# A two-product feed-forward kernel: both products read their moving tile in turns from its two halves, and part of the activation moves from VectorE to ScalarE

## The chip, the cores and the metric

The kernel runs on one core of one Trainium2 chip. A core has a matrix engine (TensorE, in the profile PE, its weight loads PEld), VectorE (DVE), ScalarE (ACT), GpSimd (POOL) and SyncE (SP, which issues transfers here). The engines run their own queues in order and wait for each other by semaphores. SBUF is the working memory, PSUM the memory that TensorE writes and from which VectorE and ScalarE read. The metric is device time in microseconds for one launch.

## The reference

`x` has 8 sequences of 4096 tokens with 192 channels, 32768 tokens in all. A causal convolution of 7 taps (softmax weights, one set for each of 8 groups of channels) is followed by a feed-forward layer with 2048 hidden values:

```python
x = lightconv(x, weight)            # (32768, 192), 7 taps per channel group
h = x @ w_in                        # 192 -> 2048
g = np.where(h >= 1, h, np.where(h <= -1, 0, (h + 1) ** 2 / 4))
out = g @ w_out                     # 2048 -> 192
```

With c = min(max(h, -1), 1), g is max(h, ((c + 1) / 2)^2). The same g comes out of min(relu((h + 1) / 2)^2, 1), and then the larger of that and h.

## The kernel before

The tokens are cut into 64 tiles of 512 (`TB`), and the hidden values into 8 groups of 256 (`NPAIR`). A step `q` is one tile `s` and one group `j` (q = 8 s + j), 512 steps in all. In step q TensorE gets the first product of q (`mm1`, into a PSUM tile `h` of 2 x 512 columns) and then the second product of q - 2 (`mm2`, into four PSUM accumulators `accm0`, `accm1`, `accr0`, `accr1`, which collect over the eight groups of a tile). Hidden values lie on the partitions, tokens are the columns, and the weights are the stationary operand.

From tile 2 on, every operand is split into a rounded part and a remainder, both fp32r (`hi`, `lo` of x; `gh`, `gl` of g; two parts of each weight). The products of the parts are summed in PSUM. The 192 channels are 128 and 64: the tiles with `r` in their names hold the last 64. Each matmul uses 64 of the 128 rows, and matmuls for the upper and the lower 64 rows stand alternately. A step has 18 matmuls of `mm1` and 20 of `mm2`, each with 512 moving columns. Tiles 0 and 1 differ: tile 0 uses plain f32 for the first product while the weights are still being split, tile 1 fp32r; the second product of both runs as `mm2_first` in f32 with 192 moving columns.

Between the products stand, for a step q:

- `act_clip` (VectorE, PSUM to SBUF): the clip to -1 and 1, into a tile `g`,
- `act_square` (ScalarE): ((c + 1) / 2)^2 in place,
- `act_max` (VectorE): the maximum with h, after which h's buffer (there are two) is free,
- `act_hi` (ScalarE) and `act_lo` (VectorE), issued in step q + 1: the rounded part `gh` and the remainder `gl`.

`both_square` and `most` form g in another way, and tile 0 uses them (part of its first step aside): a relu and a square on ScalarE, and one VectorE instruction for the minimum with 1 and the maximum with h.

After the eighth group of a tile, `evac` copies the four accumulators to SBUF on ScalarE (tiles `t`), GpSimd adds them in pairs into `sum`, `evac_rest` folds the upper and lower half of the 64 last channels, and `store` transposes blocks of 32 on VectorE and sends them out. `evac_last` does the last tile with transposes on TensorE. The accumulators have one buffer each. Beside all this the convolution of coming tiles is spread over the steps (`conv_slot`, by hand-written plans): products with the taps on ScalarE (L219), sums on GpSimd (L230), transposes on VectorE (L147).

The order on every engine is the order of the code: the schedule is manual, and the main loop writes it out.

Of the kernel before, what the change touches and what calls it, by code (L numbers as in the profile page):

```python
# [13 lines left out]
AF = mybir.ActivationFunctionType  # L14
# [4 lines left out]
P = 128  # L19
TB = 512  # L20
# [10 lines left out]
def lightconv_then_ffn(ctx: ExitStack, tc: tile.TileContext, x, weight, w_in, w_out, out):  # L31
# [24 lines left out]
    nc = tc.nc  # L56
    B, S, D = x.shape
# [7 lines left out]
    NPAIR = NF // 2  # L65
    DR = D - P
    NG = TB // SQ + 1
    TOP, BOT = slice(0, DR), slice(DR, P)
    HALVES = (TOP, BOT)
# [62 lines left out]
    NF32 = 2 * NPAIR  # L132
# [169 lines left out]
    ident = const.tile([P, P], F32, name="ident")  # L302
# [87 lines left out]
    NQ = NSB * NPAIR  # L390
    hs, g32, gs, ghs, gls, accs = {}, {}, {}, {}, {}, {}

    def mm1(q):

        s, j = divmod(q, NPAIR)

        if q == 0:
            h = hs[q] = [ps_o.tile([P, TB], F32, name=n) for n in ("accr1", "accm0")]
        else:
            h = hs[q] = ps_h.tile([P, 2, TB], F32, name="h")  # L400
            h = [h[:, e, :] for e in range(2)]

        if s == 0:
            mms = [(WI[j], us, [xop[s][u] for u in us]) for us in ("ns", "sn", "rr")]
        else:
            mms = [(W[j][:, part], u + u, [xop[s][u, x]] * 2) for u in "nsr"
                   for part, x in ((0, "hi"), (1, "hi"), (0, "lo"))]
        for n, (w, us, x) in enumerate(mms):
            for e in range(2):
                c0 = COL[us[e]][e]  # L410
                nc.tensor.matmul(h[e], w[HALVES[e], c0:c0 + P], x[e][e],  # L411
                                 start=(n == 0), stop=(n == len(mms) - 1))

    def new_accs(s):
        accs[s] = {(a, i): ps_o.tile([P, TB], F32, name=f"acc{a}{i}")
                   for a in "mr" for i in range(2)}
# [16 lines left out]
    def mm2(q):  # L433

        s, j = divmod(q, NPAIR)
        gh, gl = ghs.pop(q), gls.pop(q)
        w, wr, k = W[j + LAG], WR[j + LAG], n_in[j + LAG]
        if j == 0:
            new_accs(s)
        m0, m1, r0, r1, r = ("m", 0, gh), ("m", 1, gh), ("m", 0, gl), ("r", 0, gh), ("r", 0, gl)  # L440
        mms = [(e, m) for ms in ((m0, m1), (r0,), (r1,), (r,)) for e in range(2) for m in ms]
        if q == NQ - 1:
            mms = [(0, m) for m in (r1, m0, m1, r, r0)] + [(1, m) for m in (r1, r, m0, m1, r0)]
        first = {a: min(n for n, (e, m) in enumerate(mms) if m[0] == a) for a in "mr"}
        last = {a: max(n for n, (e, m) in enumerate(mms) if m[0] == a) for a in "mr"}
        for n, (e, (a, part, g)) in enumerate(mms):
            c0 = k + e * P
            for i in range(2):
                st = (w[HALVES[i], part, c0:c0 + P] if a == "m"
                      else wr[HALVES[i], e].rearrange("p a d -> p (a d)"))  # L450
                nc.tensor.matmul(accs[s][a, i], st, g[HALVES[i], e, :],  # L451
                                 start=(j == 0 and n == first[a]),
                                 stop=(j == NPAIR - 1 and n == last[a]))


    def tiles(q):
        return [slice(0, 1), slice(1, 2)] if q == NQ - 1 else [slice(0, 2)]

    def act_clip(q):
        g = gs[q] = act.tile([P, 2, TB], F32, name="g", bufs=3)  # L460
        for e in tiles(q):
            nc.vector.tensor_scalar(out=g[:, e, :], in0=hs[q][:, e, :], scalar1=-1.0, scalar2=1.0,  # L462
                                    op0=ALU.max, op1=ALU.min)

    def act_square(q):
        g = gs[q]
        for e in tiles(q):
            nc.scalar.activation(g[:, e, :], g[:, e, :], AF.Square, bias=0.5, scale=0.5)  # L468

    def act_max(q):  # L470
        h, g = hs.pop(q), gs[q]
        for e in tiles(q):
            nc.vector.tensor_tensor(out=g[:, e, :], in0=h[:, e, :], in1=g[:, e, :], op=ALU.max)  # L473
        if q < NF32:
            g32[q] = gs.pop(q)
# [14 lines left out]
    def evac(s):  # L490

        acc = accs.pop(s)
        n = slice(0, 2 * D if s * NPAIR < NF32 else TB)
        for a in "mr":
            t = [ob.tile([P, TB], F32, name="t", bufs=4) for _ in range(2)]
            y = ob.tile([P, TB], F32, name="sum")
            nc.scalar.copy(t[0][:, n], acc[a, 0][:, n])
            nc.scalar.copy(t[1][:, n], acc[a, 1][:, n])  # L498
            if s > 0:
                nc.gpsimd.tensor_add(y[:, n], t[0][:, n], t[1][:, n])  # L500
            else:
                late.append((y[:, n], t[0][:, n], t[1][:, n]))
            sums[s, a] = y
# [32 lines left out]
    def evac_last(s):  # L536


        acc = accs.pop(s)
        half, rest = slice(0, TB // 2), slice(TB // 2, TB)  # L540
        part = {}
        for a in "rm":
            u, v = [ob.tile([P, TB], F32, name="t", bufs=4) for _ in range(2)]
            for n in (half, rest):
                nc.scalar.copy(u[:, n], acc[a, 0][:, n])
                nc.vector.tensor_tensor(out=v[:, n], in0=acc[a, 1][:, n], in1=u[:, n], op=ALU.add)
            part[a] = v
        ps = [ps_h.tile([P, 2, TB], F32, name="h")[:, 0] for _ in range(2)]
        ps += [ps_o.tile([P, TB], F32, name=f"accr{i}") for i in range(2)]
        y = [ob.tile([P, TB], F32, name="sum") for _ in range(2)]  # L550
        for b in range(TB // P):
            nc.tensor.matmul(ps[b][:, P:D], part["r"][:, b * P:(b + 1) * P], ident[:, 0:DR],  # L552
                             start=True, stop=True)
        for i in range(2):
            for b in (2 * i, 2 * i + 1):
                nc.tensor.transpose(ps[b][:, 0:P], part["m"][:, b * P:(b + 1) * P], plain)
            for b, copy in ((2 * i, nc.scalar.copy), (2 * i + 1, nc.vector.tensor_copy)):
                copy(y[i][:, b % 2 * D:(b % 2 + 1) * D], ps[b][:, 0:D])
                if i == 1:
                    (nc.sync if b % 2 else nc.scalar).dma_start(  # L560
                        out=out[s * TB + b * P:s * TB + (b + 1) * P],
                        in_=y[i][:, b % 2 * D:(b % 2 + 1) * D])
            if i == 0:
                nc.sync.dma_start(
                    out=out[s * TB:s * TB + 2 * P].rearrange("(b p) d -> p b d", p=P),
                    in_=y[i][:, 0:2 * D].rearrange("p (b d) -> p b d", b=2))
# [180 lines left out]
    def most(h, g):  # L747

        nc.vector.scalar_tensor_tensor(out=g, in0=g, scalar=1.0, in1=h, op0=ALU.min, op1=ALU.max)
# [75 lines left out]
    for q in range(NQ + DELAY):  # L825
        s, j = divmod(q, NPAIR)
        c, i = divmod(q, 2 * NPAIR)
# [11 lines left out]
        if q < NQ:  # L839
            mm1(q)  # L840
# [7 lines left out]
        else:  # L848
            if q - 1 in gs:
                act_hi(q - 1)  # L850
            if q == NPAIR + 1:
                evac(0)
            if q == 2 * NPAIR - 2:
                pending.extend(late)
            if q < NQ:
                let_go()
                act_clip(q)
                act_square(q)
            if done % NPAIR == NPAIR - 1 and done >= NPAIR:
                (evac if done < NQ - 1 else evac_last)(done // NPAIR)  # L860
# [4 lines left out]
            if q < NQ:  # L865
                let_go()
                act_max(q)
                parts_lo(q, (False,))
                conv_slot(i, conv_b, conv_n.get("a"), conv_n.get("r"))

            m, r = (DELAY, DELAY + 1) if s > 1 else (NPAIR - 2, NPAIR - 1)
# [7 lines left out]
        if q == NQ - 4:  # L879
            plain = ob.tile([P, TB // SQ, SQ], F32, name="osb").rearrange("p j b -> p (j b)")[:, 0:P]  # L880
# [27 lines left out]
```

## Time and profile before

| | |
|---|---|
| runs | 2235.05 us median of 3 (2235.0 to 2235.06) |
| profiled execution | span 2233.2 us from first to last instruction; the page gives no other time of its own, and the median of the runs is 1.85 us above it |
| TensorE busy | 2227.3 us (100%), 19646 matmuls |
| VectorE busy | 2093.3 us (94%) |
| ScalarE busy | 1693.7 us (76%) |
| GpSimd busy | 1173.8 us (53%) |
| DMA | 110.84 MB, mean 50 GB/s |

Busy time is the union of an engine's instructions. Since matmuls overlap and their ends are modelled, the length of a matmul is better read from the starts of two groups than from a row's mean. The page's part on the chain follows, from the last instruction back, what each step waited for.

### The profile page before, as it was taken

To read this page: it belongs to the slowest core of one execution; us is meant where nothing else is said; L and a number is where in the kernel's file an instruction comes from. 1 tells how busy PE (TensorE), PEld (TensorE's weight loads), DVE (VectorE), ACT (ScalarE), POOL (GpSimd) and SP (SyncE) were. 2 spreads that over 40 slices of the span, in tenths; PEclk is the share of its full clock that TensorE was granted. 3 is DMA by queue.
4 is the path that set the end of the run, shared out by engine and by line. 5 is a ranking of instruction groups with operands and counts; after the bars stand their busy time and mean duration, and the time that the engine had idled before them with its cause. 6 is when DMAs were issued, how large, how long until landed. Compare 5 with 4: busy or idle time off the path is not lost.

```text
span 2233.2 us, 48204 instructions
## 1 busy us (share of the span) xinstructions
PE 2227.3 (100%) x19646; PEld 1850.7 (83%) x19646; DVE 2093.3 (94%) x1883; ACT 1693.7 (76%) x2153; POOL 1173.8 (53%) x868
## 2 busy tenths in 40 slices
PE   9999999999999999999999999999999999999999
PEld 6988888888888888888888888888888888888887
DVE  8899999999999999999999999999999999999998
ACT  7677877778777787777877777877778777787775
POOL 1456644556545565455664456644556545565451
PEclk9999999999999999999999999999999999999999
DMA  6222222221222212222122222222221222212211
GB/s 160 49 52 48 42 47 47 52 53 39 52 49 46 54 34 52 49 49 51 40 47 48 49 51 50 41 49 46 50 54 39 52 49 46 54 34 52 49 34 25
DMA packets 442125, 110.84 MB, mean 50 GB/s; under 512 B 410288, under 2 KB 417840, under 8 KB 441904
## 3 DMA queue, kind: packets, MB, share of 16 engines
q1 hardware_dynamic: 441744, 107.66, 24.5%
q8 instruction: 155, 2.54, 0.5%
q14 instruction: 66, 0.54, 0.1%
q10 hardware_dynamic: 160, 0.10, 0.0%
HBM read 32.84 MB, written 25.17 MB: 26 GB/s over the span
## 4 chain that ended last, share of the span: by engine, by line
PE 99%; ACT 0%; DMA 0%; DVE 0%; issue 0%; DVEq 0%; ACTq 0%
PE h L411 47%; PE accm L451 30%; PE accr L451 20%; PE accr L429 1%; PE accm L429 1%; PE accr L190 0%; PE accr L411 0%; DMA osb<-in_weight_dram 0%; PE accm L181 0%; PE h L552 0%; ACT xT L168 0%; ACT xT L165 0%; ACT xT L167 0%; PE accm L411 0%; PE h L155 0%
## 5 line engine op out<-in xcount | busy, mean ns | idle before, releaser
L230 POOL TENSOR_TENSOR y<-y,p 128x512 f32<-128x512 f32 x546 | 798.2, 1462 | 733.3 <-DVE g L473 560.7
L411 PE MATMUL h<-hi,w 64*128 64x512 f32 x4032 | 764.7, 387 | 0.0
L486 DVE TENSOR_TENSOR gl<-g,gh 128x1024 fp32r<-128x1024 f32 (+1 forms) x497 | 730.4, 1470 | 29.3 <-ACT gh L480 24.2
L468 ACT ACTIVATE g<-g 128x1024 f32<-128x1024 f32 (+1 forms) x505 | 535.5, 1061 | 234.8 <-DVE g L462 228.5
L480 ACT CAST gh<-g 128x1024 fp32r<-128x1024 f32 (+1 forms) x497 | 522.8, 1052 | 226.8 <-DVE g L473 185.2
L462 DVE TENSOR_SCALAR g<-h 128x1024 f32<-128x1024 f32 (+1 forms) x505 | 609.1, 1206 | 85.5 <-PE h L411 84.4
L451 PE MATMUL accm<-gh,w 64*128 64x512 f32 x3968 | 639.6, 387 | 0.0
L473 DVE TENSOR_TENSOR g<-h,g 128x1024 f32<-128x1024 f32 (+1 forms) x505 | 613.3, 1215 | 11.8 <-ACT g L468 4.5
L411 PEld LDWEIGHTS h<-hi,w 64*128 64x128 f32 x4032 | 561.3, 185 | 75.4
L411 PE MATMUL h<-lo,w 64*128 64x512 f32 x2016 | 613.0, 387 | 0.0
L451 PEld LDWEIGHTS accm<-gh,w 64*128 64x128 f32 x3968 | 463.6, 184 | 75.6
L451 PE MATMUL accr<-gh,wr 64*128 64x512 f32 x1984 | 414.8, 387 | 0.0
L451 PE MATMUL accr<-gl,wr 64*128 64x512 f32 x1984 | 414.8, 386 | 0.0
L451 PE MATMUL accm<-gl,w 64*128 64x512 f32 x1984 | 414.7, 387 | 0.0
L411 PEld LDWEIGHTS h<-lo,w 64*128 64x128 f32 x2016 | 371.3, 184 | 38.1 <-DMA lo<-lo 0.2
L219 ACT ACTIVATE p<-xT,wk 128x512 f32<-128x512 f32 x562 | 374.9, 709 | 0.0
L451 PEld LDWEIGHTS accm<-gl,w 64*128 64x128 f32 x1984 | 276.4, 184 | 37.9
L451 PEld LDWEIGHTS accr<-gh,wr 64*128 64x128 f32 x1984 | 276.3, 184 | 37.8
L451 PEld LDWEIGHTS accr<-gl,wr 64*128 64x128 f32 x1984 | 276.2, 184 | 37.9
L411 PE MATMUL h<-rhi,w 64*128 64x512 f32 x992 | 304.1, 386 | 0.0
L411 PE MATMUL h<-rh,w 64*128 64x512 f32 x992 | 304.1, 386 | 0.0
L500 POOL TENSOR_TENSOR sum<-t 128x512 f32<-128x512 f32 (+1 forms) x124 | 157.4, 1291 | 101.8 <-ACT t L498 101.8
(143 smaller groups left out, 1945.4 us busy)
## 6 DMA issues: line engine op xcount, KB each, us to landing
out_dram<-osb SPq DMA_DIRECT2D x366, 64.0 KB, 1.9
raw<-in_x_dram SPq DMA_DIRECT2D x334, 68.0 KB, 2.4
hi<-hi SPq DMA_DIRECT2D x126, 128.0 KB, 2.3
lo<-lo SPq DMA_DIRECT2D x126, 128.0 KB, 2.3
rhi<-rh SPq DMA_DIRECT2D x62, 128.0 KB, 2.2
rlo<-rl SPq DMA_DIRECT2D x62, 128.0 KB, 2.3
words<-in_moe_w_in_dram SPq DMA_DIRECT2D x16, 192.0 KB, 3.6
words<-in_moe_w_out_dram SPq DMA_DIRECT2D x8, 384.0 KB, 4.8
```

The source lines that it names most:

```text
L219: nc.scalar.mul(p, self.xT[:, SH + k:SH + k + TB], wk[:, self.wsel, k:k + 1])
L230: nc.gpsimd.tensor_add(y, y, self.product(k))
L411: nc.tensor.matmul(h[e], w[HALVES[e], c0:c0 + P], x[e][e], start=(n == 0), stop=(n == len(mms) - 1))
L429: nc.tensor.matmul(accs[s][a, i][:, c0:c0 + D], g[half, e, b * P:(b + 1) * P], w[half, e, :], start=(j == 0 and e == 0 and b % 2 == 0), st ...
L451: nc.tensor.matmul(accs[s][a, i], st, g[HALVES[i], e, :], start=(j == 0 and n == first[a]), stop=(j == NPAIR - 1 and n == last[a]))
L462: nc.vector.tensor_scalar(out=g[:, e, :], in0=hs[q][:, e, :], scalar1=-1.0, scalar2=1.0, op0=ALU.max, op1=ALU.min)
L468: nc.scalar.activation(g[:, e, :], g[:, e, :], AF.Square, bias=0.5, scale=0.5)
L473: nc.vector.tensor_tensor(out=g[:, e, :], in0=h[:, e, :], in1=g[:, e, :], op=ALU.max)
L480: nc.scalar.copy(gh[:, e, :], gs[q][:, e, :])
L486: eng.tensor_sub(gl[:, e, :], g[:, e, :], gh[:, e, :])
L500: nc.gpsimd.tensor_add(y[:, n], t[0][:, n], t[1][:, n])
```

## The change

Two things are done together.

First, the moving operand. `turns` views the 512 columns of a tile as two halves of 256 and takes column 0 of the first, column 0 of the second, column 1 of the first, and so on. The output is still written in order, so its columns stand in that mixed order. `mm1` does this from tile 2 on, `mm2` for every tile from 2 on. After both products a column n = 4 a + 2 b + o of an accumulator is token 256 b + 128 o + a, and `evac` writes it back to its place: it reads the PSUM columns in order and writes each to its token's column in `t`, 128 columns apart from one to the next. For the last tile, the transposes in `evac_last` take every fourth column instead.

Second, the activation. In steps 3, 4 and 11 to 15 of every sixteen (from tile 2 on, without the last two steps) ScalarE forms relu((h + 1) / 2) and its square, and VectorE one `most`, in place of clip, square and maximum.

```diff
+    def turns(t):
+        return t.rearrange("p (o c) -> p c o", o=2)
+    def both(t):
+        return t.rearrange("p (c o) -> p c o", o=2)
+    def in_turns(s):
+        return s * NPAIR >= NF32
...
     def mm1(q):
-                nc.tensor.matmul(h[e], w[HALVES[e], c0:c0 + P], x[e][e],
+                to, of = (both(h[e]), turns(x[e][e])) if in_turns(s) else (h[e], x[e][e])
+                nc.tensor.matmul(to, w[HALVES[e], c0:c0 + P], of,
...
     def mm2(q):
-                nc.tensor.matmul(accs[s][a, i], st, g[HALVES[i], e, :],
+                nc.tensor.matmul(both(accs[s][a, i]), st, turns(g[HALVES[i], e, :]),
...
+    BY_ACT = (3, 4, 11, 12, 13, 14, 15)
+    def by_act(q):
+        return q % (2 * NPAIR) in BY_ACT and NF32 <= q < NQ - 2
     def act_clip(q):
         g = gs[q] = act.tile([P, 2, TB], F32, name="g", bufs=3)
+        if by_act(q):
+            nc.scalar.activation(g, hs[q], AF.Relu, bias=0.5, scale=0.5)
+            return
...
     def act_square(q):
+        if by_act(q):
+            nc.scalar.activation(g, g, AF.Square)
+            return
...
     def act_max(q):
-        for e in tiles(q):
+        if by_act(q):
+            most(h, g)
+        for e in () if by_act(q) else tiles(q):
...
     def evac(s):
-            nc.scalar.copy(t[0][:, n], acc[a, 0][:, n])
-            nc.scalar.copy(t[1][:, n], acc[a, 1][:, n])
+            for i in range(2):
+                to, of = t[i][:, n], acc[a, i][:, n]
+                if in_turns(s):
+                    to = to.rearrange("p (b o a) -> p a b o", b=2, o=2)
+                    of = of.rearrange("p (a b o) -> p a b o", b=2, o=2)
+                nc.scalar.copy(to, of)
...
     def evac_last(s):
-            nc.tensor.matmul(ps[b][:, P:D], part["r"][:, b * P:(b + 1) * P], ident[:, 0:DR],
+            nc.tensor.matmul(ps[b][:, P:D], part["r"][:, b::TB // P], ident[:, 0:DR],
...
-                nc.tensor.transpose(ps[b][:, 0:P], part["m"][:, b * P:(b + 1) * P], plain)
+                nc.tensor.transpose(ps[b][:, 0:P], part["m"][:, b::TB // P], plain)
```

TensorE, GpSimd and SyncE keep their instructions in the same order. On ScalarE, around an evacuation in the middle of the kernel, stood before (the four copies of the accumulators in step 9 of sixteen, then the rounding to `gh`, the square, two conv products and the fold of the `r` sum in step 10, then step 11):

```order
L497 COPY t<-accm_14124 128x512
L498 COPY t<-accm_14125 128x512
L497 COPY t<-accr_14126 128x512
L498 COPY t<-accr_14127 128x512
L480 CAST gh<-g 128x1024
L468 ACTIVATE g<-g 128x1024
L219 ACTIVATE p<-xT,wk 128x512 x2
L510 COPY t<-sum 64x512
L480 CAST gh<-g 128x1024
L468 ACTIVATE g<-g 128x1024
L219 ACTIVATE p<-xT,wk 128x512 x2
```

And now, at the same place (line numbers are those of the changed kernel; L479 is the relu, L488 its square):

```order
L527 COPY t<-accm_14124 128x128x4
L527 COPY t<-accm_14125 128x128x4
L527 COPY t<-accr_14126 128x128x4
L527 COPY t<-accr_14127 128x128x4
L505 CAST gh<-g 128x1024
L491 ACTIVATE g<-g 128x1024
L219 ACTIVATE p<-xT,wk 128x512 x2
L539 COPY t<-sum 64x512
L505 CAST gh<-g 128x1024
L479 ACTIVATE g<-h 128x1024
L488 ACTIVATE g<-g 128x1024
L219 ACTIVATE p<-xT,wk 128x512 x2
```

The copies write four interleaved pieces of 128 columns, and in step 11 the relu stands between the rounding and the square; it reads `h`, and so waits for the first product itself.

On VectorE, from the end of step 10 (the transpose of the `m` sum that `store` issues) to step 12, stood before the clip (L462), the remainder (L486) and the maximum (L473) of each step:

```order
L523 STREAM_TRANSPOSE osb<-sum 128x512
L462 TENSOR_SCALAR g<-h 128x1024
L486 TENSOR_TENSOR gl<-g,gh 128x1024
L473 TENSOR_TENSOR g<-h,g 128x1024
L523 STREAM_TRANSPOSE osb<-sum 64x512
L462 TENSOR_SCALAR g<-h 128x1024
L486 TENSOR_TENSOR gl<-g,gh 128x1024
L473 TENSOR_TENSOR g<-h,g 128x1024
```

And now:

```order
L552 STREAM_TRANSPOSE osb<-sum 128x512
L511 TENSOR_TENSOR gl<-g,gh 128x1024
L778 SCALAR_TENSOR_TENSOR g<-g,h 128x1024
L552 STREAM_TRANSPOSE osb<-sum 64x512
L511 TENSOR_TENSOR gl<-g,gh 128x1024
L778 SCALAR_TENSOR_TENSOR g<-g,h 128x1024
```

The clip is gone from these steps, and one instruction of the form of `most` stands where the maximum stood. There are 215 such steps.

## The prediction

> **What bounds the kernel now.** I read the page first, then the granted clock, then the chain in order of time, then the matmuls' starts, and last the engines that might come to wait. From the page:
>
> ```profile
> span 2233.2 us, 48204 instructions
> PE 2227.3 (100%) x19646; PEld 1850.7 (83%) x19646; DVE 2093.3 (94%) x1883; ACT 1693.7 (76%) x2153; POOL 1173.8 (53%) x868
> PE 99%; ACT 0%; DMA 0%; DVE 0%; issue 0%; DVEq 0%; ACTq 0%
> ```
>
> TensorE carries 99% of the chain that ended last. VectorE is 94% busy, though, so a faster TensorE could soon wait for it. The view of cores gives the clock, the chain in order of time gives the length of a step (one step is 18 matmuls of the first product, L411, then 12 and 8 of the second, L451):
>
> ```profile
> core 0: 2233.2 us, clock 1.000
> 268.10 2.04 PE h L411 x18
> 270.14 1.36 PE accm L451 x12
> 271.50 0.91 PE accr L451 x8
> ...
> 281.02 2.04 PE h L411 x18
> ```
>
> The clock is never throttled, so nothing is to be won there. Three steps take 281.02 - 268.10 = 12.92 us, one 4.307 us. A step has 38 matmuls of 64 rows, which run as 19 pairs side by side (upper and lower half of the array): 4307 / 19 = 226.7 ns for a pair. TensorE's instructions follow each other without a gap; only the length of a pair is left to shorten.
>
> How long would a pair have to be? The first tile's steps use plain f32 operands in place of the rounded ones (fp32r), and the timeline of TensorE there shows:
>
> ```profile
> 33.08 1.91 PE L411 MATMUL h<-hi,gl 64*128 64x512 f32 x8
> 34.79 1.05 PE L411 MATMUL h<-rh,gl 64*128 64x512 f32 x4
> 35.65 0.85 PE L429 MATMUL accm<-wf,g 64*128 64x192 f32 x8
> ...
> 38.25 1.91 PE L411 MATMUL h<-hi,gl 64*128 64x512 f32 x8
> 39.97 1.05 PE L411 MATMUL h<-rh,gl 64*128 64x512 f32 x4
> 40.83 0.85 PE L429 MATMUL accm<-wf,g 64*128 64x192 f32 x8
> ```
>
> Twelve matmuls of 512 columns (six pairs) take 35.65 - 33.08 = 2.57 and 40.83 - 38.25 = 2.58 us: 429.2 ns a pair. Thirty-two of 192 columns (four rows of eight, 16 pairs) take 38.25 - 35.65 = 2.60 us: 162.5 ns a pair. The difference of 266.7 ns over 320 columns is 0.833 ns a column, and 429.2 - 512 x 0.833 leaves 2.5 ns fixed. So f32 spends two time slots of 0.4167 ns on a column. An fp32r pair, at one slot a column, should take 512 x 0.4167 + 2.5 = 215.8 ns. It takes 226.7: a surcharge of 10.9 ns, or about one slot in 20, that f32 does not pay.
>
> **The change part by part.**
>
> *Reading in turns.* Instructions, columns and stationary operands stay; only the order in which a pair fetches its 512 moving columns changes (0, 256, 1, 257, ...). It concerns 496 steps (16 to 511). Rows by form fix the count:
>
> ```profile
> L411 PE MATMUL h<-hi,w 64*128 64x512 f32 x4032 | 764.7, 387 | 0.0
> L451 PE MATMUL accm<-gh,w 64*128 64x512 f32 x3968 | 639.6, 387 | 0.0
> ```
>
> Eight of these second rows belong to a step: 3968 / 8 = 496. (The first row has 8 x 8 more, in tile 1, which stay as they are.) So 496 x 19 = 9424 pairs change. No row shows a moving operand read in turns, so I bound its pair. From below, 215.8 ns: one slot a column. From above, 429.2 ns, the f32 pair, as if each fetch needed both slots. I take 215.8. In turns each half of the tile is walked at one column every two slots, which is the pace per stream at which the f32 rows, the nearest that read 64x512 f32 data, pay no surcharge. That argument is not proof: the trace doesn't say whether f32 fetches a column once for two slots or twice at full pace. If it's the latter, the surcharge is a matter of fp32r itself and stays. Saving: 9424 x 10.9 ns = 102.7 us.
>
> *What a shorter step asks of VectorE and ScalarE.* The new step is 19 x 215.8 = 4.100 us, sixteen of them 65.6 us. Busy time over sixteen old steps, and the forms that change (the relu, its square and the combined min and max stand in the first tile's rows):
>
> ```profile
> 1000.00:1068.90 68.90, 68.90 (x612) 57.08 (x610) 65.20 (x57) 52.74 (x67) 37.86 (x30) 1.00 0.25 48
> L462 DVE TENSOR_SCALAR g<-h 128x1024 f32<-128x1024 f32 x503 | 607.9, 1208 | 84.8 <-PE h L411 83.7
> L473 DVE TENSOR_TENSOR g<-h,g 128x1024 f32<-128x1024 f32 x503 | 612.0, 1217 | 11.8 <-ACT g L468 4.5
> L749 DVE SCALAR_TENSOR_TENSOR g<-g,h 128x1024 f32<-128x1024 f32 x7 | 8.5, 1214 | 0.0
> L742 ACT ACTIVATE g<-h 128x1024 f32<-128x1024 f32 x7 | 7.1, 1014 | 2.4 <-PE h L411 2.4
> L744 ACT ACTIVATE g<-g 128x1024 f32<-128x1024 f32 x7 | 7.3, 1047 | 0.0
> ```
>
> The columns of the first row are TensorE, weight loads, VectorE, ScalarE, GpSimd. VectorE's 65.20 us would fill 99% of 65.6: without relief it would take over as the bound. In seven of sixteen steps a clip (1.208) and a maximum (1.217) become one instruction (1.214), 1.21 us less each: 65.20 - 7 x 1.21 = 56.7 us, 86%. ScalarE gains a relu of 1.014 seven times while its square stays about as it was: 52.74 + 7.1 = 59.8 us, 91%. Both fit under TensorE. The relu heads ScalarE's queue ahead of the square, the conv products and the next rounding; it waits for the first product as the clip did, and is 0.19 us shorter than the clip, so the chain product, square, maximum gets no longer. The work taken from VectorE was itself hidden; alone it moves the end by nothing.
>
> *Evacuation.* Four ScalarE copies per tile read PSUM in order but now write every 128th element of the tile in turn, 61 times (tiles 2 to 62). The timeline at one evacuation, ScalarE and TensorE:
>
> ```profile
> 1060.59 0.57 ACT L497 COPY t<-accm 128x512 f32<-128x512 f32 x1
> 1061.05 0.59 ACT L498 COPY t<-accm 128x512 f32<-128x512 f32 x1
> 1061.53 0.60 ACT L497 COPY t<-accr 128x512 f32<-128x512 f32 x1
> 1062.00 0.61 ACT L498 COPY t<-accr 128x512 f32<-128x512 f32 x1
> 1062.19 1.29 PE L451 MATMUL accm<-gh,w 64*128 64x512 f32 x8
> 1063.55 0.84 PE L451 MATMUL accr<-gh,wr 64*128 64x512 f32 x4
> L345 ACT ACTIVATE m<-words 128x768 f32<-128x768 f32 x4 | 3.7, 914 | 0.0
> ```
>
> The accumulators have one buffer, so TensorE may write accm again once the second copy ends (1061.64, 0.55 us ahead of 1062.19), and accr once the fourth ends (1062.61, 0.94 ahead of 1063.55). With steps 5% shorter about 0.45 and 0.78 are left. A longer copy, by d each, bites when 2d exceeds 0.45 or 4d exceeds 0.78: from about d = 0.2. No strided write stands in the trace. Lower bound nothing, upper bound twice the copy, d = 0.59; the nearest row is L345, which reads every second word: 914 ns for 768 columns, against about 800 on the line between the copies' 0.59 us (512) and the relu's 1.014 (1024). That is 0.15 ns a column, or d = 0.08 here: hidden. I take that, cost 0.
>
> *The tail* (the last tile's transposes read every fourth column as stationary operand) is eight small instructions: 0. DMAs, GpSimd and both queues keep their order and their work.
>
> *Sum.* By the profiled span: 2233.2 - 102.7 = 2130.5 us; the median of the runs is 1.85 us above the span, which gives **2132 us** by the runs.
>
> **The rivals.**
>
> *A. Fetching in turns is itself slow* (the other side). Place: each of the 9424 pairs. For it: every fp32r row walks consecutive columns, and none jumps 1 KB at each step; against it, only the argument of pace above. Price: with the f32 pair as the end, 9424 x (429.2 - 226.7) = +1908 us, 4143 us. It decides as soon as a pair in turns needs more than 226.7 ns, 0.44 ns a column. [...] No row here shows a strided fetch by TensorE.
>
> *B. The surcharge has nothing to do with the moving order.* It may be fixed per fp32r matmul, or sit in the write to PSUM, or in the weight loads. Then a pair stays at 226.7, and the time at 2235. Against the weights speak the f32 rows of 192 columns: they too have two loads of 64x128 to a pair and go at 162.5 ns. [...] For a fixed or PSUM cost, that every fp32r row has 512 columns, so proportional and fixed can't be told apart.
>
> *C. The gain comes, and the evacuation takes part of it back.* With d at its upper bound of 0.59, TensorE waits 4 x 0.59 - 0.78 = 1.58 us at each of 61 evacuations: 96 us, which gives 2132 + 96 = 2228. Beyond d = 0.62 even this ends slower. A surcharge that is only halved would give 2132 + 51 = 2183, in the same band.
>
> **How the numbers follow.** Forecast (2118 to 2150): 0.60, since the surcharge is real, its size is exact, and the covers hold on paper. C and partial gains (2150 to 2230): 0.14. B, within 0.2% of 2235 (about what a measurement of this kernel can tell): 0.08, low because a cost paid at one slot and not at two points at a rate. Slower: 0.18, A with 0.15 and an evacuation beyond its decisive d with 0.03. Faster is 0.60 + 0.14 = 0.74. The range from 2118 to 2240 takes in the forecast, C and B, 0.82 less a little for edges; it leaves out A. Its lower end allows a step some 14 us better in sum than the slots give.
>
> **What would show it.** Starts of L411 rows 4.10 us apart in steps 16 to 511, with the first two tiles' steps unchanged, show the reading right; 4.31 shows B, longer without any wait shows A. The evacuation copies' mean near 0.67 us shows the estimate right; a wait of the accumulators' first matmuls for ScalarE shows C. VectorE near 56.7 us and ScalarE near 59.8 in sixteen steps show the transfer. The forecast is wrong if the pair in turns is not shorter, or if ScalarE, at 91%, falls behind the first product so that TensorE waits for the maximum.

## The result and the profile after

| | median of the runs, us | lowest to highest | ratio to before, 95% interval |
|---|---|---|---|
| before | 2235.06 (4 runs) | 2235.00 to 2235.51 | |
| changed | 2292.82 (4 runs) | 2292.46 to 2292.87 | 1.0258 [1.0243, 1.0272] |

The changed kernel is 57.8 us slower, where 2132 us was forecast. From its page:

```profile
span 2291.1 us, 47743 instructions
PE 2195.7 (96%) x19646; PEld 1871.7 (82%) x19646; DVE 1859.4 (81%) x1668; ACT 1980.3 (86%) x2368; POOL 1190.7 (52%) x868
ACT 51%; DVE 15%; POOL 12%; issue 11%; PE 7%; SPq 2%; DMA 1%; POOLq 0%; DVEq 0%; ACTq 0%
```

The third line is the share of each engine in the chain that ended last. It was TensorE at 99%; now it is ScalarE at 51%, with TensorE at 7%, although no engine's busy share tells of it: ScalarE is busy 86% of the span. The timeline of TensorE around the evacuation in step 1 of sixteen follows. ScalarE issues its copies in step 1; TensorE is by then in its step 2, from 1013.63 on, in which the sums of the next tile begin (the numbers are start, length, engine, line, tiles, and in brackets the idle time before it with its releaser):

```profile
1013.63 0.62 PE L422 MATMUL h<-hi,w 64*128 64x512 f32 x4
...
1016.62 0.48 PE L462 MATMUL accm<-gh,w 64*128 64x512 f32 x1 [0.86 <-ACT t L527]
1017.51 1.13 PE L462 MATMUL accm<-gh,w 64*128 64x512 f32 x7 [0.41 <-ACT t L527]
1019.33 0.70 PE L462 MATMUL accr<-gh,wr 64*128 64x512 f32 x3 [0.25 <-ACT t L527]
1020.08 0.80 PE L422 MATMUL h<-hi,w 64*128 64x512 f32 x4
1024.18 0.80 PE L422 MATMUL h<-hi,w 64*128 64x512 f32 x4
...
1032.38 0.81 PE L422 MATMUL h<-hi,w 64*128 64x512 f32 x4
```

Two things are seen here. Where nothing waits, three steps take 1032.38 - 1020.08 = 12.30 us, 4.10 each: that is the forecast step, and a pair of 215.8 ns. And the step that meets the evacuation takes 1020.08 - 1013.63 = 6.45 us, 2.35 more, since TensorE waits three times for the copies out of the accumulators (L527). The view of waits gives how often:

```profile
DVE gl L511 <- ACT gh L505: 294.7, 306, 2.1
ACT gh L505 <- DVE g L778: 144.0, 124, 1.4
PEld accm L462 <- ACT t L527: 116.3, 121, 1.3
PE accm L462 <- ACT t L527: 73.9, 120, 0.9
PE accr L462 <- ACT t L527: 15.4, 61, 0.3
```

The third column counts waits: 120 for `accm` are two at nearly each of 61 evacuations, 61 for `accr` one at each. (Idle time is counted from the modelled end of the matmul before, so these rows undercount what a step loses: the three brackets above add up to 1.52 us of the 2.35.) Two evacuations stand in sixteen steps, of 6.45 and 6.38 us; with 0.6 us more in the steps beside them, sixteen steps take 70.84 us in place of 65.60. The loss of 5.24 is more than the 68.90 - 65.60 = 3.30 that was gained, and (5.24 - 3.30) x 31 = 60 us is the result within 3 us.

### The profile page after: what moved, and what is told of

It is laid out like the page before. It is cut to its first block, busy times and chain, and to the rows that moved or that the text cites. A ratio compares the mean times of both kernels' runs of the same rounds, so it can differ in the third digit from the quotient of the medians.

```text
span 2291.1 us, 47743 instructions
## 1 busy us (share of the span) xinstructions
PE 2195.7 (96%) x19646; PEld 1871.7 (82%) x19646; DVE 1859.4 (81%) x1668; ACT 1980.3 (86%) x2368; POOL 1190.7 (52%) x868
## 4 chain that ended last, share of the span: by engine, by line
ACT 51%; DVE 15%; POOL 12%; issue 11%; PE 7%; SPq 2%; DMA 1%; POOLq 0%; DVEq 0%; ACTq 0%
ACT gh L505 13%; POOL y L230 11%; ACT g L488 9%; ACT t L527 8%; ACT g L479 8%; DVE g L778 8%; ACT g L491 5%; ACT p L219 5%; PE h L422 3%; DVE g L482 3%; DVE g L498 2%; POOL lo L252 2%; ACT t L539 2%; DVE gl L511 1%; SPq L95 1%
## 5 line engine op out<-in xcount | busy, mean ns | idle before, releaser
L422 PE MATMUL h<-hi,w 64*128 64x512 f32 x4032 | 694.1, 378 | 0.0
L462 PE MATMUL accm<-gh,w 64*128 64x512 f32 x3968 | 612.1, 381 | 74.0 <-ACT t L527 73.9
L505 ACT CAST gh<-g 128x1024 fp32r<-128x1024 f32 (+1 forms) x497 | 519.1, 1045 | 184.5 <-DVE g L778 144.0
L462 PEld LDWEIGHTS accm<-gh,w 64*128 64x128 f32 x3968 | 443.8, 186 | 161.4 <-ACT t L527 116.3
L422 PEld LDWEIGHTS h<-hi,w 64*128 64x128 f32 x4032 | 503.1, 186 | 50.1 <-DVE g L778 0.2
L422 PE MATMUL h<-lo,w 64*128 64x512 f32 x2016 | 522.4, 376 | 0.0
L462 PE MATMUL accr<-gh,wr 64*128 64x512 f32 x1984 | 384.1, 382 | 15.4 <-ACT t L527 15.4
L462 PE MATMUL accm<-gl,w 64*128 64x512 f32 x1984 | 376.5, 383 | 0.0
L462 PE MATMUL accr<-gl,wr 64*128 64x512 f32 x1984 | 367.8, 376 | 0.0
L491 ACT ACTIVATE g<-g 128x1024 f32<-128x1024 f32 x290 | 305.8, 1055 | 58.0 <-DVE g L482 55.2
L498 DVE TENSOR_TENSOR g<-h,g 128x1024 f32<-128x1024 f32 x290 | 351.0, 1211 | 4.5 <-ACT g L491 4.2
L778 DVE SCALAR_TENSOR_TENSOR g<-g,h 128x1024 f32<-128x1024 f32 x222 | 270.3, 1218 | 102.6 <-ACT g L488 102.6
L482 DVE TENSOR_SCALAR g<-h 128x1024 f32<-128x1024 f32 x290 | 347.6, 1199 | 5.8 <-PE h L422 5.8
L422 PEld LDWEIGHTS h<-lo,w 64*128 64x128 f32 x2016 | 314.1, 186 | 23.0 <-DMA lo<-lo 0.3
L462 PEld LDWEIGHTS accr<-gh,wr 64*128 64x128 f32 x1984 | 246.6, 186 | 62.6 <-ACT t L527 39.9
L462 PEld LDWEIGHTS accm<-gl,w 64*128 64x128 f32 x1984 | 244.3, 186 | 39.2 <-DVE gl L511 16.1
L462 PEld LDWEIGHTS accr<-gl,wr 64*128 64x128 f32 x1984 | 251.5, 186 | 26.0 <-DVE gl L511 0.2
```

The costliest lines, as they stand in the source:

```text
L422: nc.tensor.matmul(to, w[HALVES[e], c0:c0 + P], of, start=(n == 0), stop=(n == len(mms) - 1))
L462: nc.tensor.matmul(both(accs[s][a, i]), st, turns(g[HALVES[i], e, :]), start=(j == 0 and n == first[a]), stop=(j == NPAIR - 1 and n == las ...
L505: nc.scalar.copy(gh[:, e, :], gs[q][:, e, :])
```

## The experiments

All ratios are to the kernel before, run beside each on the same chip. Its medians are 2234.8 to 2235.2 us throughout, so times of different runs can be subtracted to about 0.4 us.

### The parts alone

The turns alone, with the activation as before:

```diff
-    BY_ACT = (3, 4, 11, 12, 13, 14, 15)
+    BY_ACT = ()
```

> The changed kernel with the activation as before in all steps; turns and the scattered copies stay. Theory T (the 2.3 us lost at each of 61 evacuations are two things together: copies that take 0.86 us in place of 0.47, and copies that start 1.4 us later against TensorE's steps because the activation chain is behind): VectorE, 65.2 us of work in a step group of 65.6, is at least as late as the relu steps made it, so 2260 to 2320. Rival U (the scattered copies alone make the loss): about 2290, as the changed kernel. Rival V (the relu steps make it: rounding, relu, square, minimum and maximum form a ring of 4.34 us per step against TensorE's 4.10): without them only the longer copies remain, about 0.7 us each, 2132 + 61 x 0.7 = 2175.

Measured: 2262.75 us, ratio 1.0122 [1.0107, 1.0137]: the low end of theory T; U and V are out.

The seven relu steps alone, all columns in order:

```diff
-        return s * NPAIR >= NF32
+        return False
```

(with `mm2` and `evac_last` as before)

> The changed kernel with both products reading straight and plain copies; only the activation's seven steps stay. Theory T: TensorE needs 4.307 us a step, the ring of 4.34 falls behind by 0.03 us a step and the slack of the buffers takes it: 2235 to 2245. Rival U: 2235. Rival V: the relu steps are the loss, so clearly slower, 2280 or more.

Measured: 2235.48 us, ratio 1.000 [0.999, 1.001], as T and U had it.

The change with the copies of `evac` in order:

```diff
-                    to = to.rearrange("p (b o a) -> p a b o", b=2, o=2)
-                    of = of.rearrange("p (a b o) -> p a b o", b=2, o=2)
```

> The changed kernel whose copies of the accumulators write in order, so the tokens of tiles 2 to 62 leave in the mixed order (the return to token order is left out). Theory T: the copies still start late, but end 1.6 us earlier; about 0.5 us remains at each of 61 evacuations and about 0.6 us in sixteen steps elsewhere: 2160 to 2190. Rival U: the whole loss is gone, 2132 to 2140. Rival V: still about 2290.

Measured: 2207.83 us, ratio 0.9876 [0.9862, 0.9891]. The time lies outside all three forecasts: without the scattered writes more remains than T allowed.

And with the stride on the other side of the copy, so that the tokens still come to their places: PSUM is read at every fourth column, SBUF written in order.

```diff
-                    to = to.rearrange("p (b o a) -> p a b o", b=2, o=2)
-                    of = of.rearrange("p (a b o) -> p a b o", b=2, o=2)
+                    to = to.rearrange("p (b o a) -> p (b o) a", b=2, o=2)
+                    of = of.rearrange("p (a c) -> p c a", c=4)
```

> The changed kernel whose copies return to token order on the reading side: they read every fourth column of the accumulator in PSUM and write SBUF in order. Theory T and rival U: if a read with a step of 16 bytes from PSUM costs nothing, as the run with plain copies (T 2160 to 2190, U 2132 to 2140); if it costs what the scattered writes do (0.86 us a copy), 2290 as the changed kernel. Rival V: 2290 in either case.

Measured: 2208.20 us, ratio 0.9878 [0.9863, 0.9893], the time of the copies in order, and so again outside the three forecasts.

The relu steps do nothing at the old length of a step. The scattered writes of the copies cost 2292.82 - 2208.20 = 84.6 us, and all of that goes when the same permutation is done on the reading side. The copies' rows by form, first of the changed kernel, then with the strided read (busy total, and mean ns of one):

```profile
L527 ACT COPY t<-accr 128x512 f32<-128x512 f32 x122 | 122.8, 1110 | 0.0
L527 ACT COPY t<-accm 128x512 f32<-128x512 f32 x122 | 117.7, 1066 | 0.0
```

```profile
L527 ACT COPY t<-accr 128x512 f32<-128x512 f32 x122 | 66.1, 601 | 0.0
L527 ACT COPY t<-accm 128x512 f32<-128x512 f32 x122 | 64.2, 576 | 0.0
```

Still, 2208 is 76 us above the forecast, and the relu steps, which should relieve VectorE, were the next to look at.

### The relu's place in ScalarE's queue

The strided read without any relu step:

```diff
-    BY_ACT = (3, 4, 11, 12, 13, 14, 15)
+    BY_ACT = ()
```

> Turns and copies that return to token order on the reading side, with the activation as before in every step. Theory R (what is left, 76 us above 2132, is lateness of the activation chain at the evacuations; in the first of the two in sixteen steps it comes from the ring rounding, relu, square, minimum and maximum, 4.34 us a step against 4.10): without the relu steps VectorE has 65.2 us of work for 65.6, so it is late in its own way: 2185 to 2215, near the 2208 with the relu steps. Rival D (the relu steps pay for themselves, VectorE would be the bound without them): 2225 or more, VectorE over 97% busy.

Measured: 2170.40 us, ratio 0.9711 [0.9696, 0.9725], below both forecasts. So with short steps the relu steps are a loss of 37.8 us as they stand. The chain in order of time, in the changed kernel's steps 11 to 15, shows why:

```profile
999.37 1.23 DVE g L778
1000.62 1.06 ACT gh L505
1001.68 0.93 ACT g L479
1002.63 1.06 ACT g L488
1003.72 1.23 DVE g L778
1004.97 1.04 ACT gh L505
```

The rounding of step q - 1 (L505) waits for the minimum and maximum of that step (L778). The relu of step q (L479) stands behind the rounding on ScalarE's queue, then come its square (L488) and, on VectorE, the next L778. Each waits for the one before, the relu only for its turn on the queue: a ring that turns once a step and takes 1003.72 - 999.37 = 4.35 us. At the old step of 4.31 us it hardly matters, which fits the 2235.48 of the relu steps alone; at 4.10 us every such step falls 0.25 us behind, and five of them in a row, 11 to 15, come just ahead of the evacuation in step 1. The relu needs only the first product, not the rounding; so it was put ahead, with the strided read kept:

```diff
+            early = q < NQ and by_act(q)
+            if early:
+                act_clip(q)
             if q - 1 in gs:
                 act_hi(q - 1)
...
-                act_clip(q)
+                if not early:
+                    act_clip(q)
                 act_square(q)
```

> The same with the seven relu steps, but ScalarE issues the relu of step q ahead of the rounding of step q - 1. Theory R: the ring is cut, since the relu then waits for the first product alone; the stretched steps (0.44 us in sixteen) and the lateness at the first evacuation (0.87 us) go: 2208 - 31 x 1.3 = 2168, within 2155 to 2180. Rival D (VectorE's load in the steps with transposes sets the lateness at both evacuations): 2195 to 2210.

Measured: 2156.45 us, ratio 0.9649 [0.9633, 0.9665], as theory R had it: the fastest kernel of this study and 78.6 us under the one before. The timeline of ScalarE there:

```profile
1006.30 1.02 ACT L479 ACTIVATE g<-h 128x1024 f32<-128x1024 f32 x1 [0.64 <-PE h L422]
1007.24 1.04 ACT L505 CAST gh<-g 128x1024 fp32r<-128x1024 f32 x1
1008.19 1.05 ACT L488 ACTIVATE g<-g 128x1024 f32<-128x1024 f32 x1
...
1010.40 1.02 ACT L479 ACTIVATE g<-h 128x1024 f32<-128x1024 f32 x1 [0.65 <-PE h L422]
```

The relu now waits for the first product, and comes every 4.10 us: TensorE sets the pace again, with 100% of the chain that ended last. (Without the relu the ring is some 4.35 - 0.95 = 3.4 us, an estimate from the pieces above.) The same move with the scattered copies of the changed kernel left in place (the edit above, without the strided read):

> The changed kernel with one edit: ScalarE issues the relu of step q ahead of the rounding of step q - 1; the scattered copies stay. Theory R (the ring of 4.34 us a step is a cause of its own, beside the scattered copies): as with the read-side copies, where the order gained 52 us, the first of the two evacuations in sixteen steps starts on time: 2225 to 2255. Rival (with the copies at 0.86 us ScalarE stays late at each evacuation whatever the order): 2280 to 2293.

Measured: 2245.93 us, ratio 1.0049 [1.0034, 1.0064], as theory R had it. That fills a table:

| us | no relu steps | relu behind the rounding | relu ahead of it |
|---|---|---|---|
| scattered write | 2262.75 | 2292.82 | 2245.93 |
| strided read | 2170.40 | 2208.20 | 2156.45 |
| difference | 92.4 | 84.6 | 89.5 |

The scattered copies cost 85 to 92 us in every column, and the relu's place 46.9 or 51.7 us in either row. The two add up to within 4.9 us; they do not multiply.

### The scattered copies without short steps

The kernel before, with nothing but the scattered write in `evac`, from tile 2 on (its two copies become one loop, as in the change):

```diff
+                if s * NPAIR >= NF32:
+                    to = to.rearrange("p (b o a) -> p a b o", b=2, o=2)
+                    of = of.rearrange("p (a b o) -> p a b o", b=2, o=2)
                 nc.scalar.copy(to, of)
```

> The kernel before with nothing but the scattered copies (the products read straight, so the tokens of tiles 2 to 62 leave in a wrong order). Theory T (two causes that multiply): the copies take 0.86 us in place of 0.47, but start on time, so only 4 x 0.39 - 0.94 = 0.62 us is lost at an evacuation: 2235 + 61 x 0.62 = 2273 at most, 2245 to 2275. Rival U (the scattered copies alone make the loss of 2.3 us): 2235 + 61 x 1.8 = 2345.

Measured: 2308.73 us, ratio 1.033 [1.0315, 1.0346]: 73.7 us, 1.2 us for each of 61 evacuations, with steps at their old length. That lies between theory T and rival U, inside neither. The timeline at the two evacuations of one sixteen, that of step 1 and that of step 9 (ScalarE and TensorE; L411 starts a step, L451 is the second product):

```profile
1022.09 0.82 PE L411 MATMUL h<-hi,w 64*128 64x512 f32 x4
1022.51 2.00 ACT L502 COPY t<-accm 128x512 f32<-128x512 f32 x2
1024.31 2.06 ACT L502 COPY t<-accr 128x512 f32<-128x512 f32 x2
1027.24 0.85 PE L411 MATMUL h<-hi,w 64*128 64x512 f32 x4
...
1057.40 0.84 PE L411 MATMUL h<-hi,w 64*128 64x512 f32 x4
1058.55 1.98 ACT L502 COPY t<-accm 128x512 f32<-128x512 f32 x2
1060.33 2.05 ACT L502 COPY t<-accr 128x512 f32<-128x512 f32 x2
1060.58 1.19 PE L451 MATMUL accm<-gh,w 64*128 64x512 f32 x7 [0.40 <-ACT t L502]
1063.24 0.85 PE L411 MATMUL h<-hi,w 64*128 64x512 f32 x4
```

A copy starts about 0.9 us after the one before ((1024.31 - 1022.51) / 2 and (1060.33 - 1058.55) / 2), 0.47 in the prediction's rows. At the first of the two evacuations the copies start 0.42 us into TensorE's step, as punctually as before (0.44: 1060.59, step at 1060.15). The step takes 1027.24 - 1022.09 = 5.15 us and loses 0.84, near the 4 x 0.43 - 0.94 = 0.78 that theory T works out. At the second they start 1.15 us in, and the step loses 1063.24 - 1057.40 - 4.31 = 1.53. So T's formula holds where the copies start on time, and being 0.73 us later costs 0.69 more. Why ScalarE comes late to the second evacuation even at the old step no run shows by itself.

### How far apart may neighbours be read?

The turns jump 1 KB at each fetch and yet save 10.9 ns a pair (215.8 in place of 226.7). To see what stride does cost, the second product alone was made to read every other column (8 bytes apart), first the even ones, then the odd ones; `mm1` stays in turns, the copies and `evac_last` are plain:

```diff
-                nc.tensor.matmul(both(accs[s][a, i]), st, turns(g[HALVES[i], e, :]),
+                nc.tensor.matmul(accs[s][a, i].rearrange("p (o c) -> p o c", o=2), st,
+                                 g[HALVES[i], e, :].rearrange("p (c o) -> p o c", o=2),
```

> The first product reads in turns; the second reads every other column of g (0, 2, 4, ..., then 1, 3, 5, ...; a step of 8 bytes), which returns the tokens to their order, so the copies are plain. Theory F (the surcharge belongs to fetching neighbouring columns one after another): the second product's pair is 215.8 ns, the time as with plain copies, 2208. Rival H (two walks 1 KB apart are what helps): the second product's pair stays at 226.7, or gets longer; 4960 x 10.9 ns = 54 us more work, partly covered by the lateness: 2215 to 2265, and 2300 upwards if a step of 8 bytes costs extra.

Measured: 3302.78 us, ratio 1.4778 [1.4756, 1.4801].

```profile
1000.35 0.75 PE L422 MATMUL h<-hi,w 64*128 64x512 f32 x4
1002.31 2.11 PE L462 MATMUL accm<-gh,w 64*128 64x512 f32 x8
1006.80 0.76 PE L422 MATMUL h<-hi,w 64*128 64x512 f32 x4
```

The first product keeps its 9 pairs in 1.96 us, about 218 ns a pair, and the 10 pairs of the second take 1006.80 - 1002.31 = 4.49 us, 449 ns each, with no wait among them: 2.1 times the pair in turns. Theory F fell: its 215.8 ns became 449. The time is where rival H put a step of 8 bytes that costs extra.

### Three attempts at the last 24 us

At 2156.45 the fastest kernel is 24 us above the forecast. In sixteen steps one still runs long, the one in which TensorE meets the second evacuation (that of step 9), 1062.09 - 1057.26 = 4.83 us in its timeline of TensorE and ScalarE:

```profile
1057.26 0.80 PE L422 MATMUL h<-hi,w 64*128 64x512 f32 x4
1058.94 1.05 ACT L527 COPY t<-accm 128x512 f32<-128x512 f32 x2
...
1062.09 0.80 PE L422 MATMUL h<-hi,w 64*128 64x512 f32 x4
```

0.73 us, 31 times, is 23 us. The first copy starts 1058.94 - 1057.26 = 1.68 us into the step. VectorE has hardly a gap in steps 6 to 9, where no step is relieved: its timeline names no wait between the 0.16 us ahead of the remainder of step 6, at 1045.64, and the 0.39 us ahead of that of step 10, at 1061.94. So relu steps were added there, and then moved there from 4 and 15 (both with the relu ahead and the strided read):

```diff
-    BY_ACT = (3, 4, 11, 12, 13, 14, 15)
+    BY_ACT = (3, 4, 6, 7, 11, 12, 13, 14, 15)
```

> As the run with 3, 6, 7 and 11 to 14, but nine relu steps (3, 4, 6, 7, 11 to 15). Theory D: 2133 to 2142 too, ScalarE at about 59.5 of 65.6 us. Rival S: two more relus of 1 us leave ScalarE behind, 2150 or more.

```diff
-    BY_ACT = (3, 4, 11, 12, 13, 14, 15)
+    BY_ACT = (3, 6, 7, 11, 12, 13, 14)
```

> Turns, read-side copies, relu first, and the seven relu steps at 3, 6, 7 and 11 to 14 in place of 3, 4 and 11 to 15: VectorE, which works without a gap in steps 5 to 8, gets its relief there. Theory D (what remains above 2132 is the start of the second evacuation, late because VectorE is behind in steps 5 to 8): the 0.7 us at 31 evacuations go, 2133 to 2142. Rival S (ScalarE, with conv products in these steps, makes it late instead): 2156 or more.

Measured: 2208.02 us, ratio 0.988 [0.9865, 0.9894], and 2222.13 us, ratio 0.9943 [0.9926, 0.9959]. Both are slower than without the edit, by 51.6 and 65.7 us, as rival S had it. What fell is the remedy: a relu in these steps relieves VectorE but loads ScalarE (in the first of the two runs VectorE is busy 1765.5 us and ScalarE 1915.3, against 1846.1 and 1860.6 in the fastest kernel), and in that run the first copy of the second evacuation starts 2.08 us into TensorE's step instead of 1.68. Whether VectorE's load is what makes it late in the fastest kernel, the two runs cannot tell, since both engines' loads changed. From the waits of the first of the two:

```profile
DVE gl L511 <- ACT gh L505: 408.5, 364, 2.5
...
PEld accm L462 <- DVE gl L511: 41.4, 60, 0.8
```

VectorE's remainder waits 408.5 us for ScalarE's rounding (264.9 in the fastest kernel), and TensorE's loads now wait for the remainder, of which the fastest kernel's waits have no line. In steps 6 and 7 ScalarE has two convolution products besides (1.32 us for the two); with the relu also ahead of the rounding, the rounding comes late there, and the remainders wait for it 2.18 and 1.12 us.

The last run kept the relu steps of the fastest kernel and put the four copies of step 9 ahead of the square of that step (here `i` is the step in sixteen):

```diff
                 if not early:
                     act_clip(q)
+                ahead = i == NPAIR + 1 and q >= NF32
+                if ahead:
+                    evac(done // NPAIR)
                 act_square(q)
...
-            if done % NPAIR == NPAIR - 1 and done >= NPAIR:
+            if done % NPAIR == NPAIR - 1 and done >= NPAIR and not ahead:
```

> The relu stands ahead of the rounding and the copies read PSUM every fourth column, as in the fastest run so far (2156 us). There only the evacuation in step 9 of every sixteen still costs TensorE time: that step took 4.83 us instead of 4.10, 0.73 us, 31 times = 23 us. Now in step 9 the four copies stand ahead of the square on ScalarE, instead of behind it. Theory E: the copies can start some 1.0 us earlier (the rounding ahead of them ended at 1057.95 us there, the copies started at 1058.94), which covers the 0.73 us, and the square, later by the copies' 1.9 us, is hidden by the two steps that lie between a first product and its second: 2156 - 23 = 2133 us, between 2130 and 2142. Rival V: VectorE has no idle time between steps 5 and 10 of sixteen, so its maximum, later by 1.9 us, moves the wait to the rounding and remainder of step 9 and to TensorE's loads for them: 2150 us or more, perhaps above 2156.

Measured: 2191.15 us, ratio 0.9803 [0.9787, 0.9819]: 34.7 us slower than without it, as rival V had it. The timeline of the three engines (gathered by engine):

```profile
1074.25 1.07 ACT L527 COPY t<-accm 128x512 f32<-128x512 f32 x2
1076.15 1.09 ACT L491 ACTIVATE g<-g 128x1024 f32<-128x1024 f32 x1
...
1077.27 1.22 DVE L498 TENSOR_TENSOR g<-h,g 128x1024 f32<-128x1024 f32 x1 [1.67 <-ACT g L491]
...
1078.55 0.70 PE L422 MATMUL h<-hi,w 64*128 64x512 f32 x4 [0.55 <-DVE g L498]
...
1086.56 0.70 PE L462 MATMUL accm<-gl,w 64*128 64x512 f32 x4 [0.73 <-DVE gl L511]
```

No matmul waits for a copy any more. But the square (L491) starts only at 1076.15, VectorE idles 1.67 us for it, and the maximum (L498) comes late for two others: it frees the buffer of `h`, for which the first product waits 0.55 us, and it holds up what follows on VectorE's queue, so that two steps on the second product waits 0.73 us for a remainder. The wait has been moved and has grown. What would take the last 24 us without such a trade stays open.

## Why the prediction was wrong, point by point

**Reading in turns: right in size.** The step is 4.10 us and the pair 215.8 ns, as worked out from the f32 rows. That f32 spends two slots on a column and fp32r one was the author's estimate: the traces show 0.833 ns a column for the f32 pairs and 4.10 us / 19 = 215.8 ns for the fp32r pair in turns, which fits half of that for a column and the 2.5 ns fixed, but no trace shows a slot. The argument of pace that led there, called no proof by the prediction, is not shown by any run; the size came out, the reason stays open. Rival B (a surcharge that stays) is refuted, and so is A as a statement on turns: the pair fetched from two places 1 KB apart took 215.8 ns, where consecutive columns took 226.7. Not every stride is as cheap: every other column, 8 bytes apart, took 449 ns a pair.

**Shorter steps, "the chain product, square, maximum gets no longer": the first step that failed.** The working checked busy time against 65.6 us, and by that account both engines fit. So they do in the trace of the changed kernel, in a window of 70 us, a little under its sixteen steps (TensorE, weight loads, VectorE, ScalarE, GpSimd):

```profile
1000.00:1070.00 70.00, 67.01 (x604) 57.05 (x602) 56.84 (x49) 61.41 (x72) 38.43 (x29) 1.00 0.24 47
```

VectorE 56.84 (forecast 56.7) and ScalarE 61.41 (forecast 59.8 with copies as short as before). What the working left out is the order on ScalarE. It said that the relu heads the queue ahead of the next rounding, which is so, but not that it stands behind the rounding of the step before, and that this one waits for VectorE. The ring that closes there takes 4.35 us against a step of 4.10. Cost: 46.9 to 51.7 us by the runs that move the relu, put down as 0.

The other half of this step was right in part. Without any relief VectorE takes part in setting the end, though it does not take over as the bound: the chain of that kernel has TensorE at 29% and VectorE at 23%.

```profile
1000.00:1065.60 65.60, 65.29 (x603) 57.16 (x599) 63.73 (x56) 51.12 (x65) 35.40 (x29) 1.00 0.26 50
```

That is sixteen steps of the kernel without relu steps and with the strided read (2170.40); VectorE, the third of the busy times, fills 63.73 of 65.60 us, and the relief, rightly placed, is worth 2170.40 - 2156.45 = 14 us.

**Evacuation, "I take that, cost 0": the second step that failed.** The copies became longer by d = 0.39 us between starts (0.86 against 0.47; two copies from 1015.54 to 1017.26 below), where 0.08 was taken from a row with a strided read: the term is about five times too small. The upper bound of 0.59 held. But the size explains only part: the formula with d = 0.39 gives 4 x 0.39 - 0.78 = 0.78 us an evacuation, 48 us in sum, and TensorE lost 2.35. The slack of 0.45 and 0.78 us was read at an evacuation whose first copy was punctual (the step's start and the copy's, from the kernel before). In the changed kernel it is not (the other four lines):

```profile
1060.15 0.84 PE L411 MATMUL h<-hi,w 64*128 64x512 f32 x4
1060.59 0.57 ACT L497 COPY t<-accm 128x512 f32<-128x512 f32 x1
...
1014.57 1.06 ACT L491 ACTIVATE g<-g 128x1024 f32<-128x1024 f32 x1
1015.54 1.92 ACT L527 COPY t<-accm 128x512 f32<-128x512 f32 x2
1017.26 2.01 ACT L527 COPY t<-accr 128x512 f32<-128x512 f32 x2
1019.08 1.05 ACT L505 CAST gh<-g 128x1024 fp32r<-128x1024 f32 x1
```

The step began at 1013.63, so the first copy starts 1.91 us into it, not 0.44. With this lateness put in, the formula gives (1.91 - 0.44) + 0.78 = 2.25 of the 2.35 us. The same reading from the timelines of the other kernels, one sixteen of steps each (us into TensorE's step at which the first copy starts, and the length of that step):

| kernel | evacuation of step 1 | evacuation of step 9 |
|---|---|---|
| before | 0.44, step 4.30 | 0.38, step 4.31 |
| scattered write, turns alone | 0.81, step 5.39 | 1.81, step 6.37 |
| scattered write, relu behind (changed) | 1.91, step 6.45 | 1.82, step 6.38 |
| scattered write, relu ahead | 0.70, step 5.27 | 1.81, step 6.38 |
| strided read, no relu steps | 0.84, step 4.10 | 1.80, step 4.96 |
| strided read, relu behind | 1.91, step 5.06 | 1.81, step 4.97 |
| strided read, relu ahead (fastest) | 0.70, step 4.10 | 1.68, step 4.83 |

The relu's place decides the start in step 1: behind the rounding it is about 1.1 us later than without relu steps, near the 5 x 0.25 us of the ring. In step 9 it changes the start by 0.13 us at most; there the copies start late in every kernel with short steps, and that is what the prediction's "about 0.45 and 0.78 are left" had wrong beside the size of d: with copies as short as before, a start of 0.84 us still costs nothing, and one of 1.68 costs 0.73. What makes step 9 late is not shown.

Rival C had the right place and the right direction, with "beyond d = 0.62 slower" as the point from which it decides; that point was too far out, because it too took the copies to be on time. From the table of the runs, an evacuation pays 85 to 92 us / 61 = 1.4 to 1.5 us of the 4 x 0.39 = 1.56 us that its copies take longer: next to nothing was hidden.

**The sum, made again with the measured terms.** 2235.1 - 102.7 (turns, as forecast) + 24.1 (left over in the fastest kernel, 23 of it read at the second evacuation) + 51.7 (relu behind the rounding) + 89.5 (scattered copies) - 4.9 (what the last two share) = 2292.8. The last three terms are differences between runs, the first is worked out from the step, and the 24.1 is what then remains; so the sum closes by its making and is no test of its own.

## What to carry to other kernels

Shortening the engine that bounds a kernel tests every ring through the other engines against the new step, not only their busy sums: follow one in-order queue through its waits and back to itself, and compare the length of that turn with the step. A slack read from a trace holds only as long as what stands ahead of it stays punctual; here copies that grew by 4 x 0.39 = 1.56 us paid 1.4 to 1.5 of it at each evacuation, although ScalarE was busy only 86% of the span in the changed kernel, and 79% with the turns alone. A permutation that has to be paid somewhere is best tried at every place where it can be done, since the same copy cost 85 us with the stride on one side and 0.4 us, no more than the runs can tell apart, with it on the other (2208.20 against 2207.83).

## What the hardware showed that was not expected

- TensorE's fetch of an fp32r moving operand: consecutive columns 226.7 ns for a pair of 512, two halves in turns (1 KB apart) 215.8, every other column (8 bytes apart) 449. The last is 449 / 512 = 0.88 ns a column, 2.1 times that of the pair in turns. No run shows the fetch itself, and why consecutive columns pay 10.9 ns more than columns in turns stays open.
- ScalarE's copy of 128x512 f32 from PSUM: 576 to 601 ns when it reads every fourth column (16 bytes apart) and writes in order, as long as with both sides in order (576 to 602, the run with plain copies), and 1066 to 1110 ns in the changed kernel, where it reads in order and writes every 128th column of SBUF (512 bytes apart). The slow write also has an innermost run of only four elements (128x128x4); no run separates the distance from that shape.
